# Attention by whole tiles, keys in pairs, and weights, zeros and G moved in a fused attention and mixture kernel

## The chip, the core and the metric

The kernel runs on one core of a Trainium2 chip. The metric is the device time of one execution in microseconds, the median of three runs. PE is the matmul engine, PEld its weight load, DVE the vector engine, ACT the activation engine, POOL the general engine, and SP the engine whose queue issues most of the DMA transfers.

## The reference

All data are fp32. Attention has 2 batches, 8 heads, 768 tokens a batch and 64 channels a head; a query sees 8 global keys and its own last 96, with a bias that falls with the distance. Its output is, as 1536 tokens of 512 channels, the input of a soft mixture of 8 experts with 4 slots each, and the result of that goes through a top-2 mixture of 8 experts with a noisy gate.

```python
scores = np.where(keep, scale * q @ k.T + bias, -1e9); a = softmax(scores); x = a @ v      # heads joined
logits = x @ phi                                                    # soft mixture, 32 slots
d = softmax over tokens; slot_input = d.T @ x
slot_out[e] = relu(slot_input[e] @ w1[e]) @ w2[e]                   # 512 -> 1024 -> 512
x = softmax over slots (logits) @ slot_out
noisy = x @ w_gate + log1p(exp(x @ w_noise)) * noise                # top-2 mixture
top2 = two largest of noisy, weights by softmax
out[mask] += top2_w * (relu(x[mask] @ w1[e]) @ w2[e])               # 512 -> 1024 -> 512
```

## The kernel before

**Attention** works on 12 tiles of 128 tokens. A tile has 4 pairs of heads and is done as two blocks i of two pairs. The loop of `attention_near` runs over the 24 blocks and 3 more turns; in turn i it does scores and exponentials of block i, values of block i - 2 and the turn (transposes) of block i - 1. `scores` (L206) makes four score groups of 167 columns; DVE adds the bias, takes the row's extreme and writes them to SBUF (L209, an eviction); ACT exponentiates them with their sums (`exps`, L216); `norm` adds 1e-9 to the sums on POOL (L222), inverts on DVE (L223) and scales on POOL into Pb (L231, L233); `turn` transposes Pb on PE (L241) and evicts to PT on ACT (L243); `values` multiplies with v (L257); `valued` copies the tile's result to xT on DVE (L264); `stX` transposes it back (L274, copied at L280). After tiles 3, 7, 10 and 11 `logits` (L291) and `seg` (L295 on) bring the last 4, 4, 3 and 1 tiles into a running softmax over tokens: Et, Lsb and rs, transposes at L323 and L324, matmuls at L347, and an update of the sum U (L351).

**Tail.** The last segment's softmax is joined to the others in small steps (L536 to L569): a maximum over partitions, weights Wc, the update of U, then psi = U Wc (L567, "o" in the trace) and siT, the soft experts' input.

**Soft experts.** The weights come as 32 units of 1 MB, four an expert (two of w1a, two of w2a). Units 0 to 15 are loaded in halves during attention; `more_w` with `PACE` (L371) sets how many have been issued by which turn. Units 16 to 31 follow (L616). An expert is `ffn_a` (h, L652), `ffn_t` (m, L685) and `ffn_b` (y, L698). The order of PE is h of e, then m of e - 1, then y of e - 2.

**Routing.** The output op becomes soT; the top-2 mixture doesn't build its input x but works on slots: x = c @ slot_out, so w1 of an expert is first multiplied by slot_out (`g_mm`, also L652, to "pg"; G = relu's input per soft slot), split into fp16 halves `hi` and `lo` (`g_hi` L830, `g_lo` L833), and spread over partitions (`g_mid`, L843 and L844; `g_end`). K0, K1 and K2 are the first three experts of the top-2 mixture; their G, the gate, the top-2 choice and the places of 24 slots of 128 rows are computed together, by order lists written out by hand. Between them stand matmuls without use that keep PE at work (`warm`, L722). A row table ctab with c and the gate of each token goes to DRAM from POOL's queue (L1152), and `slot_a` gathers the 128 rows of a slot from it (L1254) by an index (gidx, L1396). Slots 0 and 1 are taken directly (`direct`, L1138; `slot_h`, L1121). `slot_t` (L1025) turns the gathered rows, `slot_h` and `slot_y` (L1221) are the expert.

**Rows out.** The output is zeroed by DMA (512 rows during attention, `zero_out` L358, 1024 rows in the routing stretch, `zero` L875), and each slot is added to it by an indirect DMA (L1236).

SP's queue is in order, over 8 semaphore lanes: each transfer waits until the eighth before it has landed. In attention, the soft experts and routing PE, and in attention and routing the other engines too, run in the order in which the program is written.

## Time and profile before

| | us |
|---|---|
| median of three runs | 341.44 (339.24 to 341.98) |
| the profiled execution | 339.79 |
| its span, first to last instruction | 337.8 |
| PE busy | 316.5 (94 %) |
| ACT, DVE, POOL busy | 208.0, 197.8, 136.9 |
| granted clock of PE, mean | 0.983 |
| attention ends, experts begin | about 101, 107.46 |
| soft experts end, slot 2 begins | 143.88, 176.59 |

Times in the trace are us from the first instruction. A row of the timeline gives the start, the busy time of a run of like instructions, engine, line and operation, and in brackets the idle time before and what ended it. [...] Busy time of an engine that isn't waited for costs nothing.

### The profile page before, as it was taken

The page shows a single profiled execution, that of the slowest core. Times are in us where ns is not written, and L with a number is a line of the kernel's source. Part 1 is how long each engine was busy: PE and PEld are TensorE (multiplying, and loading weights), DVE is VectorE, ACT ScalarE, POOL GpSimd, SP SyncE. Part 2 cuts the span into 40 slices and gives each one's busy share as a digit, 9 for nine tenths or more (in the row PEclk, how much of TensorE's full clock was granted, in tenths as well). Part 3 has the DMA queues.
Part 4 walks back from the last instruction along what each step waited for, and adds up shares of the span by engine and source line. Part 5 has one row for each costly group of instructions (what it writes and reads, how often), then busy time and mean ns, then how long its engine had stood idle before and what let it go on. Part 6 is the DMA issues. An engine that isn't in the chain of part 4 may idle for free. (4 is left out here: it accounts for less than half of the span.)

```text
span 337.8 us, 7453 instructions
## 1 busy us (share of the span) xinstructions
PE 316.5 (94%) x2687; PEld 187.2 (55%) x2687; DVE 197.8 (59%) x702; ACT 208.0 (62%) x490; POOL 136.9 (41%) x192
## 2 busy tenths in 40 slices
PE   8999999999978999899979999999999999999990
PEld 3789878878854443254544554545454545544540
DVE  3755655556546200049977696797669396898110
ACT  2788868767822210059938796596878695876320
POOL 4466543644520000021444765463643534533131
PEclk9999999999997899999999999999999999999997
DMA  6999999999999999999968999959998955322353
GB/s 176 260 311 291 301 300 278 300 300 309 315 385 394 395 398 399 389 394 398 397 239 183 335 303 367 290 111 318 328 308 262 317 181 71 39 30 31 46 72 47
DMA packets 49226, 89.25 MB, mean 264 GB/s; under 512 B 3408, under 2 KB 18384, under 8 KB 49184
## 3 DMA queue, kind: packets, MB, share of 16 engines
q1 hardware_dynamic: 44704, 80.79, 73.1%
q0 software_dynamic: 4480, 7.92, 14.4%
q8 instruction: 23, 0.38, 0.5%
q14 instruction: 19, 0.16, 0.1%
HBM read 78.56 MB, written 10.14 MB: 263 GB/s over the span
## 5 line engine op out<-in xcount | busy, mean ns | idle before, releaser
L1221 PE MATMUL y<-w2hl,hh 128*128 128x512 f16 x552 | 125.3, 379 | 0.8 <-ACT w2hl L1232 0.8
L1221 PEld LDWEIGHTS <-hh 128*128 128x128 f16 x552 | 52.5, 98 | 62.4 <-issue 4.0
L216 ACT ACTIVATE Tt<-Tt,nm 128x167 f32<-128x167 f32 x96 | 40.5, 424 | 13.0 <-DVE nm L209 12.2
L1130 DVE SCALAR_TENSOR_TENSOR hh<-h,hh 128x512 f16<-128x512 f32 x46 | 29.6, 684 | 22.3 <-ACT hh L1122 22.3
L1236 POOL DMA_INDIRECT out_y<-ys,sidx x15 | 26.9, 1792 | 26.1 <-ACT ys L1230 13.0
L815 DVE SCALAR_TENSOR_TENSOR w2hl<-w,pm,w2hl 128x1024 f16<-128x1024 f32 x28 | 35.1, 1279 | 1.2 <-issue 0.7
L231 POOL TENSOR_TENSOR Pb<-Tt,r 128x668 f32<-128x668 f32 x24 | 31.2, 1300 | 9.4 <-DVE r L223 9.1
L209 DVE CUSTOM_DVE_ANT_0 Tt<-s,bias 128x167 f32<-128x167 f32 x96 | 26.3, 329 | 14.3 <-PE s L206 14.2
L1254 POOL DMA_INDIRECT cT<-ctab,gidx x25 | 28.4, 1137 | 12.8 <-DVE pm L771 6.3
L206 PE MATMUL s<-kx,qd 128*128 128x167 f32 x192 | 31.6, 307 | 0.5 <-DVE nm L209 0.2
L1122 ACT ACTIVATE hh<-h 128x512 f16<-128x512 f32 x46 | 25.0, 598 | 11.0 <-PE h L1121 11.0
L812 ACT ACTIVATE w2hl<-w,pm 128x1024 f16<-128x1024 f32 x28 | 31.3, 1150 | 0.5 <-DVE pm L771 0.5
L243 ACT ACTIVATE PT<-pt 128x512 f32<-128x512 f32 (+1 forms) x48 | 24.4, 558 | 10.4 <-PE pt L241 10.2
L783 ACT ACTIVATE w2hl<-w 128x1024 f16<-128x1024 f32 x28 | 29.5, 1058 | 1.4 <-DMA w<-in_w2b 1.4
L206 PEld LDWEIGHTS s<-kx,qd 128*128 128x128 f32 x192 | 28.0, 196 | 1.1 <-DVE nm L209 0.5
L1236 POOL DMA_INDIRECT out_y<-c,sidx x7 | 12.2, 1736 | 38.3 <-DVE gsc L1215 7.6
L241 PE MATMUL pt<-c,Pb 128*128 128x128 f32 x176 | 24.4, 280 | 1.1 <-POOL Pb L233 1.0
L257 PE MATMUL px<-PT,vt 128*64 128x128 f32 x352 | 24.5, 279 | 0.0
L241 PEld LDWEIGHTS pt<-c,Pb 128*128 128x128 f32 x176 | 18.9, 141 | 6.9 <-issue 3.0
L257 PEld LDWEIGHTS px<-PT,vt 128*64 128x64 f32 x352 | 18.8, 136 | 4.3 <-issue 3.3
L652 PE MATMUL h<-w,siT 128*32 128x256 f32 x256 | 17.4, 418 | 1.6 <-DMA w<-in_w1a 1.5
L1230 ACT ACTIVATE ys<-y,gsc 128x512 f32<-128x512 f32 x15 | 10.3, 688 | 12.9 <-PE y L1221 12.8
(295 smaller groups left out, 465.2 us busy)
## 6 DMA issues: line engine op xcount, KB each, us to landing
w<-in_w2b SPq DMA_DIRECT2D x14, 1024.0 KB, 13.3
x<-in_w1b SPq DMA_DIRECT2D x12, 1024.0 KB, 13.7
w<-in_w1a SPq DMA_DIRECT2D x16, 512.0 KB, 9.6
w<-in_w2a SPq DMA_DIRECT2D x16, 512.0 KB, 9.7
w<-in_w1a SPq DMA_DIRECT2D x8, 1024.0 KB, 13.7
w<-in_w2a SPq DMA_DIRECT2D x8, 1024.0 KB, 15.5
kx<-in_ka SPq DMA_DIRECT2D x12, 272.0 KB, 7.8
qd<-in_qt SPq DMA_DIRECT2D x24, 128.0 KB, 8.2
```

The costliest lines, as they stand in the source:

```text
L206: nc.tensor.matmul(s[:, t, :], qv[:, p, t, :], kx[:, p, a:a + 167], start=True, stop=True)
L216: nc.scalar.activation(Tt[:, k], Tt[:, k], AF.Exp, bias=nm[:, k:k + 1], scale=-1.0, accum_out=st[:, k:k + 1])
L231: nc.gpsimd.tensor_tensor(wide(Pn, 33, 264 + 64, 528, 167), Pu.rearrange("p (a t) c -> p a t c", t=2), rb(167), ALU.mult)
L241: nc.tensor.transpose(pt[:, ch, t], Pn[:, 2 * (n % 2) + t, 136 * ch:136 * ch + 128], ident)
L257: nc.tensor.matmul(px[64 * h:64 * h + 64, p, :], vv[:, c:c + 64], PT[:, ch, :, 64 * h:64 * h + 64], start=(ch == 0 or m == 0), stop=(ch == 1))
L783: nc.scalar.activation(w2hl[:, self.r, 1, 2 * q:2 * q + 2], self.quarter(q), AF.Abs, accum_out=self.wm[:, q:q + 1])
L812: nc.scalar.activation(w2hl[:, self.r, 0, 2 * q:2 * q + 2], self.quarter(q), AF.Copy, scale=self.sw)
L815: nc.vector.scalar_tensor_tensor(w2hl[:, self.r, 1, 2 * q:2 * q + 2], self.quarter(q), self.sw, w2hl[:, self.r, 0, 2 * q:2 * q + 2], ALU.m ...
L1130: nc.vector.scalar_tensor_tensor(hh[:, 1, 4 * q:4 * q + 4], phs[q], 0.0, hh[:, 0, 4 * q:4 * q + 4], ALU.max, ALU.subtract)
L1221: nc.tensor.matmul(py, hh[:, hx, f], w2hl[:, e, wx, f], start=(n == 0), stop=(n == 23))
L1236: o = nc.gpsimd.indirect_dma_start(out=out, out_offset=bass.IndirectOffsetOnAxis(ap=sidx[:, j:j + 1], axis=0), in_=ys, in_offset=None, com ...
L1254: nc.gpsimd.indirect_dma_start(out=cgf[:, place(n)], out_offset=None, in_=ctab, in_offset=bass.IndirectOffsetOnAxis(ap=gidx[:, n:n + 1], a ...
```

## The change

1. The attention loop runs over whole tiles T. Within a tile, the two blocks' scores and exponentials are done, and ACT's evictions of the transposes of tile T - 1 stand one by one among the exponentials (`turn(..., True)` hands back the eviction). The values of tile T - 1 follow at the tile's end. PT has 4 buffers for 2. r is computed on DVE.
2. Keys of tiles 2 to 11 come in pairs of tiles, so rows of 1088 B for 544 B. Values are loaded a tile later.
3. w2a and w2b are read with two rows of weights in a row (4 KB per partition for 2 KB); the halves of h are laid out to match.
4. No zeros are written in attention; one late transfer from 128 partitions writes all 1536 rows (512 and 1024 rows from 64 partitions before).
5. The constants of the first load are cut to 260 columns; the rest comes with the gate's weights and the noise in one later load.
6. In the tail the last tile's part is added to psi in PSUM by four matmuls instead of through U; all engines run in written order; three warming matmuls are added. The splitting of c into fp16 (`halves`) moves into the soft experts.
7. In routing K1's G is computed whole before the first place where G is used, in the bank of K0's; K2's G moves up to the direct slots; the table is written from SP's queue, with the loads of K2's w2b behind it.

```diff
-PACE = lambda i: 1 + 4 * i // 3
+PACE = lambda i: 1 + 3 * i // 2
...
-        w2r = d["w2a"].rearrange("e (c p) f -> e p c f", p=128)
+        w2r = d["w2a"].rearrange("e (c p i) f -> e p c (i f)", p=128, i=2)
...
-        def load_k(T):
+        def load_k(T, n=1):
             a = KP + KS * (T % 6)
-            nc.sync.dma_start(out=kx[:, :, a:a + KS], in_=d["ka"][T].rearrange("p (a t) -> p a t", a=4))
+            nc.sync.dma_start(out=kx[:, :, a:a + n * KS], in_=d["ka"][T // 2][:, :, KS * (T % 2):KS * (T % 2 + n)])
...
-            nc.gpsimd.tensor_scalar(r, st, 1e-9, None, ALU.add)
+            nc.vector.tensor_scalar(r, st, 1e-9, None, ALU.add)
...
-            PT = lo.tile([128, 2, 2, 128], F32, name="PT", bufs=2)
-            nc.scalar.activation(PT[:, c0:], pt[:, c0:], AF.Copy)
-            X["PT", n] = PT
+            PT = X["PT", n] = lo.tile([128, 2, 2, 128], F32, name="PT", bufs=4)
+
+            def out():
+                nc.scalar.activation(PT[:, c0:], pt[:, c0:], AF.Copy)
+
+            if later:
+                return out
+            out()
...
+            for T in range(NT + 1):
+                new, b0, b1 = T < NT, 2 * T, 2 * T + 1
...
                 if new:
-                    more_w(PACE(i))
-                s1 = segs.get(T - 2) if u else None
+                    more_w(PACE(b0))
+                    st0, nm = [sm.tile([128, 4], F32, name=k, bufs=3) for k in ("st", "nm")]
+                    scores(b0, nm)
+                    exps(b0, st0, nm, (0, 1))
...
+                outs = [turn(n, True) for n in (2 * b0 - 4, 2 * b0 - 3)] if T else []
+                for k, o in enumerate(outs):
+                    o()
+                    if new:
+                        exps(b0, st0, nm, (2 + k,))
...
+                    scores(b1, nm)
+                    norm(b0, st0)
+                    exps(b1, st, nm, (0,))
...
+                outs = [turn(n, True) for n in (2 * b1 - 4, 2 * b1 - 3)] if T else []
+                for k, o in enumerate(outs):
+                    o()
+                    if new:
+                        exps(b1, st, nm, (1 + k,))
+                if new:
+                    exps(b1, st, nm, (3,) if outs else (1, 2, 3))
...
+                if T:
+                    for n in range(2 * b0 - 4, 2 * b0):
                         values(n)
...
+        def joined(c):
+            nc.tensor.matmul(psi[:, c, :], U[:, 128 * c:128 * c + 128], Wc, start=(c == 0), stop=False)
...
         for c in range(4):
-            tc.keep_in_program_order(nc.tensor.matmul(psi[:, c, :], U[:, 128 * c:128 * c + 128], Wc, start=True, stop=True))
-        warm(2)
...
+            nc.tensor.matmul(psi[:, c, :], xl[:, 128 * c:128 * c + 128], Ek[:, P1], start=False, stop=(c == 3))
...
         def zero(a, b):
-            nc.sync.dma_start(out=out[a:b].rearrange("(p t) c -> p t c", p=64),
-                              in_=zt[0:64].unsqueeze(1).to_broadcast([64, (b - a) // 64, 512]))
+            nc.sync.dma_start(out=out[a:b].rearrange("(p t) c -> p t c", p=128),
+                              in_=zt.unsqueeze(1).to_broadcast([128, (b - a) // 128, 512]))
...
-        warm(5)
+        warm(2)
+        K1.g_mm(of=K0)
...
-        K1.g_mm((0, 1))
...
-            nc.gpsimd.dma_start(out=ctab.rearrange("(p t) c -> p t c", p=128), in_=crow.bitcast(F32))
+            nc.sync.dma_start(out=ctab.rearrange("(p t) c -> p t c", p=128), in_=crow.bitcast(F32))
+            K2.u.update({i: load_part(2, i, part(stage, i)) for i in (2, 3)})
...
         pct = direct(z)
+        K1.g_pow_a()
+        K2.g_mm((0, 1), of=K0)
...
         h0 = slot_h(0, t01[:, 0:128], scratch([128, 2, 8, 128], F16))
-        K1.g_mm((2, 3))
+        K2.g_mm((2, 3))
...
-        zero(ZREST, NTOK)
+        zero(0, NTOK)
...
-        K1.g_pow_b()
-        K1.g_hi()
-        K1.g_lo()
-        K2.g_mm()
         K1.g_out(0, pm_([128, 2, 256]))
```

ACT in attention, before, two tiles' blocks in the middle (Tt holds a block's scores, nm its row extremes, st its sums, pt the transposes):

```order
L216 ACTIVATE Tt_971,st_969<-Tt_971,nm_970 128x167 x4
L243 ACTIVATE PT_999<-pt_994 128x512
L243 ACTIVATE PT_1006<-pt_1001 128x512
L216 ACTIVATE Tt_1021,st_1019<-Tt_1021,nm_1020 128x167 x4
L243 ACTIVATE PT_1056<-pt_1051 128x512
L243 ACTIVATE PT_1063<-pt_1058 128x512
```

The same engine after, one tile (the blocks 1002 and 1034):

```order
L209 ACTIVATE Tt_1002,st_1000<-Tt_1002,nm_1001 128x167 x2
L238 ACTIVATE PT_1020<-pt_1015 128x512
L209 ACTIVATE Tt_1002,st_1000<-Tt_1002,nm_1001 128x167
L238 ACTIVATE PT_1026<-pt_1021 128x512
L209 ACTIVATE Tt_1002,st_1000<-Tt_1002,nm_1001 128x167
L209 ACTIVATE Tt_1034,st_1032<-Tt_1034,nm_1033 128x167
L238 ACTIVATE PT_1056<-pt_1051 128x512
L209 ACTIVATE Tt_1034,st_1032<-Tt_1034,nm_1033 128x167
L238 ACTIVATE PT_1062<-pt_1057 128x512
L209 ACTIVATE Tt_1034,st_1032<-Tt_1034,nm_1033 128x167 x2
```

The pair of evictions after four exponentials has become four single evictions, each between two exponentials.

SP's queue in routing, before (w2hl<-in_w1b and in_w2b are K2's units, c the row table's tile; the table is on POOL's queue here):

```order
L667 DMA w_1990<-in_w2b 128x4x512
L667 DMA w_1992<-in_w2b 128x4x512
L667 DMA x_2019<-in_w1b 128x2x1024
L667 DMA x_2021<-in_w1b 128x2x1024
L667 DMA w_2065<-in_w2b 128x4x512
L667 DMA w_2067<-in_w2b 128x4x512
L667 DMA w2hl<-in_w1b 128x2x1024 x2
L667 DMA w2hl<-in_w2b 128x4x512 x2
L1403 TENSOR_LOAD go
```

SP's queue there after:

```order
L718 DMA w_1986<-in_w2b 128x2x1024
L718 DMA w_1988<-in_w2b 128x2x1024
L718 DMA x_2015<-in_w1b 128x2x1024
L718 DMA x_2017<-in_w1b 128x2x1024
L718 DMA w2hl<-in_w1b 128x2x1024 x2
L718 DMA w_2064<-in_w2b 128x2x1024
L718 DMA w_2066<-in_w2b 128x2x1024
L1210 DMA ctab<-c_1688 128x864
L718 DMA w2hl<-in_w2b 128x2x1024 x2
L1466 TENSOR_LOAD go
```

K2's w1b units are ahead of K1's w2b now, and the table stands between K1's and K2's w2b; SP waits there until the table's tile is written.

PE between slot 1's values and slot 2's transpose, before (pg is G, the rows L843 and L844 are K1's g_mid):

```order
L1221 MATMUL y<-w2hl,hh 128x512
L652 MATMUL pg<-w2hl,soT 32x256 x16
L843 LDWEIGHTS w2hl
L843 MATMUL m<-ghi,w2hl 128x256
L844 LDWEIGHTS w2hl
```

PE there after:

```order
L1284 MATMUL y<-w2hl,hh 128x512
L901 LDWEIGHTS w2hl
L901 MATMUL m<-ghi,w2hl 128x256
L902 LDWEIGHTS w2hl
L902 MATMUL m<-glo,w2hl 128x256
```

The 16 matmuls of K2's G (twice that in the trace) are gone from this place; they stand in two halves of 8 around `slot_h` of slot 0.

## Rows read from the trace of the kernel before

**Rows 1.** PE's row of the page: busy tenths in 40 equal slices of the span.

```profile
PE   8999999999978999899979999999999999999990
```

**Rows 2.** Windows: us, length, busy time (instructions) by engine, clock, DMA share, GB/s.

```profile
32.58:39.40 6.82, 6.82 (x70) 6.13 (x69) 3.85 (x20) 5.64 (x21) 4.04 (x7) 1.00 1.12 302
...
100.00:110.00 10.00, 9.04 (x57) 5.26 (x58) 6.27 (x21) 1.82 (x6) 0.81 (x3) 0.74 1.04 397
```

**Rows 3.** Timeline of a plain tile, ACT, then DVE: start, length, line, idle before.

```profile
33.90 0.43 ACT L216 ACTIVATE Tt<-Tt,nm 128x167 f32<-128x167 f32 x1 [0.41 <-DVE nm L209]
...
36.04 1.08 ACT L243 ACTIVATE PT<-pt 128x512 f32<-128x512 f32 x2 [0.35 <-PE pt L241]
...
33.47 0.33 DVE L209 CUSTOM_DVE_ANT_0 Tt<-s,bias 128x167 f32<-128x167 f32 x1 [0.46 <-PE s L206]
...
36.02 0.18 DVE L223 RECIPROCAL r<-r 128x4 f32<-128x4 f32 x1 [0.85 <-POOL r L222]
...
38.59 0.69 DVE L264 COPY xT<-px 128x512 f32<-128x512 f32 x1 [0.40 <-PE px L257]
```

**Rows 4.** Timeline of attention, PE: the pieces behind idle time.

```profile
45.77 0.30 PE L323 MATMUL psl<-c,Et 128*128 128x128 f32 x1 [0.42 <-DVE Lsb L320]
...
60.83 1.09 PE L241 MATMUL pt<-c,Pb 128*128 128x128 f32 x8 [0.56 <-POOL Pb L233]
...
97.83 0.27 PE L323 MATMUL psl<-c,Et 96*128 96x96 f32 x1 [1.78 <-DVE rs L326]
```

**Rows 5.** Timeline of the tail and the soft experts, PE, last its weight load.

```profile
104.77 1.91 PE L567 MATMUL o<-Wc,U 128*128 128x32 f32 x8 [0.49 <-DVE U L351]
...
107.46 5.65 PE L652 MATMUL h<-w,siT 128*32 128x256 f32 x64
...
131.69 0.44 PE L685 MATMUL m<-c,hs 128*128 128x128 f32 x2
...
136.65 1.07 PE L652 MATMUL h<-w,siT 128*32 128x256 f32 x16 [1.50 <-DMA w<-in_w1a]
...
137.65 0.44 PE L685 MATMUL m<-c,hs 128*128 128x128 f32 x2
...
140.24 3.64 PE L698 MATMUL y<-w,hT 128*32 128x512 f32 x32
...
142.41 0.13 PEld L698 LDWEIGHTS y<-w,hT 128*32 128x32 f32 x4 [0.30 <-DMA w<-in_w2a]
```

**Rows 6.** DMA packets of three stretches: 20 to 60, 110 to 140, 177 to 190 us.

```profile
DMA packets 10018, 12.07 MB, mean 302 GB/s; under 512 B 570, under 2 KB 6532, under 8 KB 10011
...
DMA packets 4714, 11.85 MB, mean 395 GB/s; under 512 B 347, under 2 KB 347, under 8 KB 4711
...
DMA packets 1286, 2.64 MB, mean 203 GB/s; under 512 B 95, under 2 KB 95, under 8 KB 1286
```

**Rows 7.** Timeline of routing and the loop, PE, with DVE and POOL for the gather.

```profile
154.89 1.24 PE L722 MATMUL y<-c 128*128 128x512 f16 x5
...
161.18 0.61 PE L1121 MATMUL h<-w2hl,Gst 128*128 128x128 f16 x8 [0.52 <-DVE w2hl L1172]
...
173.84 1.93 PE L652 MATMUL pg<-w2hl,soT 128*32 128x256 f32 x32 [1.70 <-issue]
...
176.59 0.22 PE L1025 MATMUL m<-k,cT 128*128 128x128 f16 x1
...
220.69 1.07 PE L652 MATMUL pg<-x,soT 128*32 128x256 f32 x16 [0.53 <-DMA x<-in_w1b]
...
169.42 0.17 DVE L1396 TENSOR_SCALAR gidx<-m 128x25 int32<-128x25 f32 x1
...
172.66 1.05 POOL L1254 DMA_INDIRECT cT<-ctab,gidx  x1 [6.32 <-DVE pm L771]
```

**Rows 8.** DMA issues of the page: KB each, median us from issue to landing.

```profile
out_y<-w2hl SPq DMA_DIRECT2D x1, 2048.0 KB, 12.9
...
ctab<-c POOLq DMA_DIRECT2D x1, 432.0 KB, 6.2
```

More of the change, by code (lines that the diff above doesn't have):

```diff
@@ L99, in load_unit @@
             tv = pl.tile([128, 2048], F32, name=nm, tag=nm).rearrange("p (c f) -> p c f", c=n)
-            units[k] = tv
+            units[k] = tv if not which else tv.rearrange("p c (i f) -> p (c i) f", i=2)
             c = n // parts
@@ L297, in seg @@
             P = slice(0, 32 * w)
-            last = t0 + w == NT
-            hand = near and not last
+            late = near and w < 4
             old, nm = rn
@@ L439, in attention_near @@
-                if s1:
-                    list(s1)
-                if u == 0 and T - 2 in SEGS and T - 2 < NT - 1:
-                    segs[T - 2] = seg(*SEGS[T - 2], logits(*SEGS[T - 2]))
-                if 0 <= i - 1 < NB:
-                    for n in (2 * (i - 1), 2 * (i - 1) + 1):
-                        turn(n)
-                if new:
-                    norm(i, st)
-                if u == 0 and T - 2 in segs:
-                    next(segs[T - 2])
-                    next(segs[T - 2])
@@ new lines, in attention_near @@
+                if T == 0:
+                    tables(0, 0, 2)
+                fill(FILL.get(T, 0))
+                if old:
+                    next(old)
+                if new and 0 <= T - 2:
+                    stX(T - 2)
+                if old:
+                    next(old)
+                if new and T - 2 in SEGS:
+                    segs[T - 2] = seg(*SEGS[T - 2], logits(*SEGS[T - 2]))
+                if T - 2 in SEGS:
+                    next(segs[T - 2])
+                if new:
+                    norm(b1, st)
@@ L455, in attention_near @@
             more_w(2 * (NWA + NW))
+            old = segs[T - 2]
+            fill(1, ps_t.tile([128, 512], F32, name="pt"))
+            next(old)
+            next(old)
+            fill(1, ps_t.tile([128, 512], F32, name="pt"))
             psl = logits(*SEGS[NT - 1])
+            next(old)
+            next(old)
             stX(NT - 1)
             s_hand.close()
-            return psl
+            return psl, old
         def attention_any():
@@ L538, in warm @@
             for _ in range(k):
-                tc.keep_in_program_order(nc.tensor.matmul(pw, warmw[:, 0:128], warmw[:, 0:512], start=True, stop=True))
-        steps = seg(*SEGS[NT - 1], psl)
-        next(steps)
+                nc.tensor.matmul(pw, warmw[:, 0:128], warmw[:, 0:512], start=True, stop=True)
+        s_tail = ExitStack()
+        s_tail.enter_context(tc.manual_schedule(engines=hands))
+        P1 = slice(0, 32)
+        old, nm = rn
+        nc.vector.tensor_copy(nm, old)
+        mx = sm.tile([128, 1], F32, name="mx", bufs=2)
@@ L551, in emit @@
-        next(steps)
+        nc.scalar.activation(wun, old, AF.Exp, bias=mneg, scale=-1.0)
+        nc.scalar.activation(Et[P1], psl[P1], AF.Exp, bias=mneg[P1], accum_out=sg[P1])
+        Wc = cw.tile([128, 32], F32, name="Wc")
+        nc.vector.tensor_scalar(Wc, sel4[:, 0:32], wun, None, ALU.mult)
         sw = cw.tile([128, 1], F32, name="sw")
         nc.vector.tensor_tensor(sw, wun, rs, ALU.mult)
-        Wc = cw.tile([128, 32], F32, name="Wc")
-        nc.vector.tensor_scalar(Wc, sel4[:, 0:32], wun, None, ALU.mult)
@@ L556, in emit @@
-        next(steps)
+        siT = mid.tile([128, 4, 32], F32, name="siT")
+        psi = ps_o.tile([128, 4, 32], F32, name="o")
+        def joined(c):
+            nc.tensor.matmul(psi[:, c, :], U[:, 128 * c:128 * c + 128], Wc, start=(c == 0), stop=False)
+        joined(0)
+        pe = ps_s.tile([128, 2, 128], F32, name="s")
+        nc.tensor.transpose(pe[:, 0, P1], Et[P1], ident[P1, P1])
+        nc.vector.tensor_copy(Ek[:, P1], pe[:, 0, P1])
+        nc.vector.tensor_tensor(sw[P1], sw[P1], sg[P1], ALU.add)
@@ L608, in ph_, with cut32 @@
             return ps_h.tile(shape, dt, name="h")
[L610 to L611 removed]
+        more = cs2.tile([128, 260 + NSLOT + 1], F32, name="more")
+        def cut32(a, n):
+            return more[:, a:a + n]
+        wgn = cut32(0, 64).rearrange("p (c e) -> p c e", c=4)
+        noise = cut32(64, 96).rearrange("p (t e) -> p t e", t=NT)
+        padrow, ovth, below = cut32(160, 1), cut32(161, 72).rearrange("p (e k) -> p e k", e=8), cut32(233, 8)
+        sltm, quarter, spare = cut32(241, NOV), cut32(259, 1), cut32(260, NSLOT + 1)
         for k in range(NWA + NW, 32):
@@ L909, in emit @@
         K0.g_mm()
+        K2 = raw[2] = Rank(2, {i: load_part(2, i, part(stage, i)) for i in (0, 1)})
         K1.u.update({i: load_part(1, i, ring(i)) for i in (2, 3)})
-        K2 = raw[2] = Rank(2, {i: load_part(2, i, part(stage, i)) for i in range(4)})
         warm(3)
```

243 lines of the change are left out of this document (124 added, 119 removed).

## The prediction

> **What bounds the kernel now.** I read the slices of the span first, then the windows, then single stretches of the timeline. [rows 1] show PE at nine tenths or more in nearly all 40 slices, so time is won only where PE idles, does work that need not be there, or runs at a lower clock. The windows [rows 2] say that a plain attention tile takes 6.82 us, every bit of it PE, with ACT busy 5.64 beside it. [...] So three places can give time: the idle pieces inside attention, the stretch from attention's end to the end of the soft experts (clock and data), and the routing stretch. From 185 us on PE is full and its order is the same in both kernels, so a gain made before that is kept to the end, if nothing there arrives late.
>
> **The change part by part**, against the profiled execution's own 339.79 us (span 337.8). The median of the three runs is 1.65 higher.
>
> *Attention by whole tiles.* PE's work per tile is the same, so first the idle time. In [rows 4] PE idles 0.56 for Pb from POOL (once more alike, 0.45 at 18.00), 0.42 for Lsb (once more alike at 75.43), and 1.78 before the third segment's transposes. The change puts a whole turn of the other half tile between a block's exponentials and its transposes, and the segment's steps further apart, so all 3.63 should go. In their place comes a loop on ACT and DVE. ACT's order per tile is now e e P e P e | e P e P e e (e an exponential, P an eviction of transposes), and DVE has r and its reciprocal of the second block, the xT copy, and only then the next tile's first score eviction. r waits for the last exponential, and behind it wait xT and the next evictions, for which ACT waits. Around the loop, from [rows 3]: 0.43 from the first eviction's start (33.47) to the first exponential (33.90); seven exponentials at 0.43 and four evictions at 0.50 (two take 1.08) make 5.0; the last exponential 0.52 with the read of its sum; r and reciprocal 0.42 with two hand-overs, an estimate from the reciprocal's 0.18 for each; xT 0.61 of its 0.69. Sum 6.98 against PE's 6.82. I take 0.15 more for each of the five tiles that have no logits or segment work on PE (in the others PE is longer): +0.7. The ends: nothing (PE still sets the tile) and 8.66, which is a rival below. Attention: -2.9. Moving r to DVE takes 0.22 off POOL, which has 4 of 6.82 us busy [rows 2]; nothing.
>
> *The tail.* From attention's last matmuls to the first expert the chain now runs through the update of U (PE waits 0.49 for it at 104.77) and eight instructions for psi that take 1.91, at the low clock [rows 5]. The change adds the last tile in PSUM instead: no wait for U, but four more matmuls behind the four, and three or so warming ones. -0.5, -0.95 for psi at full clock, +0.85 for what is added: -0.6. Ends: -1.4 (the additions lie beside the softmax chain) and +0.9 (the clock stays low). That the clock stays up is a choice: before it fell, PE idled 1.78 at 97.83 and did scraps of work until 104.7, and the change removes that idle piece and fills others.
>
> *Soft experts.* Now 107.46 to 143.88 (140.24 + 3.64): 36.4 us [rows 5]. The first 64 instructions take 5.65 at the low clock where 32 of the same form take 1.93 [rows 7], so 1.8 is lost. The experts' m matmuls come every 3.95 us (127.74, 131.69), so the next would come at 135.64 and came at 137.65: 2.0 of waiting for w1a, and 0.3 for the last w2a unit at 142.41. Without these 32.3: -4.1.
>
> *Is the data there?* In the new time the second half of the last expert's h matmuls needs its unit 7.0 us sooner than it now arrives (136.65), and the last quarter of the last expert 7.6 sooner than 142.41. [Rows 6] give the stream's prices: from 20 to 60 us 10018 packets carry 12.07 MB, from 110 to 140 us 4714 carry 11.85. Splitting 16 engines' time into a part per packet and a part per byte, 640 = 10018 a + 12.07 b and 480 = 4714 a + 11.85 b engine-us, a is 0.029 us. Keys: ten tiles in five pairs make 2560 packets of 1088 B of 5120 of 544 B, so 2560 x 0.029 / 16 = 4.6 us less. Early zeros: 2048 packets of 512 B cost at least their bytes (1.05 MB at 395 GB/s, 2.7 us) and at most the two-part price (5.6, with b = 0.029 us per KB); I take 3.9, since they are writes and no row has them alone. Second weights with 4 KB packets: 256 packets fewer in each of 16 units, by the two-part price 0.46 us a unit; but in the second stretch, where both kinds of unit alternate, 1 MB takes 2.65 at 395 GB/s, and the last two w2a units took 2.88 each (136.65 to 142.41, the wait's delay in it), so the difference may be small; between 0 and 0.46 I take a third, since the price comes from far smaller packets: 2.6. Together 11.1, so 3.5 to 4 to spare, and PE sets the time. [...]
>
> *Routing.* Here [rows 7]. K2.g_mm leaves its place with 1.70 of idle time before it and 1.93 of work: -3.63. K1.g_mm comes whole behind the prefix matmul (+1.93) in place of three of five warming matmuls (-0.74), and its first half leaves the place before the direct slots (-1.0). K2's first half goes behind them (+1.0), where PE idles 0.52 now. K2's second half takes the place of K1's. Sum -3.0. Late next is the gather of slot 2's rows: issued at 172.66, 3.2 us after its index (169.42), because the row table, written while four units were under way, took 6.2 to land [rows 8]. Now the table goes ahead of two of these units on SP's queue; if it takes half as long, gather 2 goes out at about 169.8 and the slot's transpose, 3.93 behind it as now, can start at 173.7 in the old time, where PE is there at 173.6. Ends: -3.6 and 0. The wait that SP takes for the table delays K2's w2b units, needed only in the expert loop; the c16 split moved into the expert stretch lies on ACT and DVE beside a PE with 3.95 us of work per expert; smaller constants: nothing to 0.2.
>
> *Late zeros and the loop.* 3.1 MB of zeros instead of 2.1, from 128 partitions. Now the 64-partition write runs at 203 GB/s [rows 6], 12.9 us to landing [rows 8]. Behind it come expert 3's units and then those for which PE waits 0.53 at 220.69 [rows 7]. At 395 GB/s the zeros take 8.0, 2.3 less than 2.1 MB at 203; at 203 they take 15.5. No row shows a large write from 128 partitions; reads into 128 partitions run at 395, so I take 8.0, and the 0.53 goes: -0.5. [...]
>
> Sum: -2.9 - 0.6 - 4.1 - 3.0 - 0.5 = -11.1: 328.7 by the profiled execution, 330.3 by the median. I put the forecast between the two: **329.5**.
>
> **The rivals** (each on the same scale).
> - The clock falls again between attention and the experts, since the tail stays a chain of small steps: 1.8 + 0.95 come back, 332.3. For: the drop now comes with just these scraps. Against: less idle time. 0.15.
> - The stream stays the bound. With nothing from the keys 6.5 of 7.6 are won: 330.6; with the low end of the other terms too (2.7 and 0) 4.9 are missing: 334.4. Packets at their bytes' price alone would do it; [rows 6] speak against. 0.12.
> - The late zeros go at 203 GB/s: 5.2 more for the units behind them, and PE waits 5.7 at the place of the 0.53: 335.2. 0.09.
> - Routing keeps its length, since the gather or DVE's chain, not PE, sets slot 2: 332.5. This is also what is left if moving G does nothing. 0.09.
> - **Slower:** the loop on ACT and DVE pays each hop. Now ACT waits 0.41 for DVE and 0.35 for PE's transposes once per half tile [rows 3]; interleaved, it can wait for PE before each of four evictions. 5.5 of work, 2 x 0.41, 4 x 0.35 and 0.94 back through r and xT make 8.66 a tile: ten tiles 18.4 later, less 3.6, the rest -8.2: 347. It ends above before from 8.0 a tile on. Against: the transposes of the tile before can be done long before their place on ACT, since four PT buffers and a step's lead stand between. 0.07.
>
> My case has 0.48; its own range is 326 to 332.5 (loop at 6.82 and the tail's lower end on one side, the gather's on the other). The other cases end at 330.6 to 335.2, so 325.5 to 336 leaves out 0.17 to 0.2. One per cent, about what runs of this kernel can tell from no change, is 338.0 to 344.9: a loop half-way to the slower rival (7.5 a tile) would still give 335, so faster 0.86, same 0.07, slower 0.07.
>
> **What would show it.** Right: PE full in plain tiles of 6.8 to 7.1 us; no 1.78 gap; the granted clock 1.00 from 100 to 120 us; no wait of PE for w1a or w2a; the experts in 32.3 us; no gap before slot 2's transpose; the zeros landing within 9 to 11 us. Wrong: a gap of PE once per tile that ends on DVE's evictions; waits for units of the first experts, because loads now hang on buffers that free themselves later; a slot that waits for its gather behind the zeros.

## Result: 335.4 us, in the range, but under half of the gain

The changed kernel takes **335.42 us** (median of four, 334.62 to 336.41), the kernel before 340.34 beside it; the ratio is 0.9866 [0.9817, 0.9914]. The forecast was 329.5, in a range of 325.5 to 336. So the direction and the range held and the size did not: 5 us came of 11.1. Ratios compare fast runs alone, and of the profiles below one, that of x12, is of a slow run.

The profiled execution (334.62, span 332.8) is 5.0 shorter than that of before, so the two traces can be laid side by side. Each line is the start of the same piece of work in both, and the gain made between it and the line above:

| | before | after | gain of the stage | forecast |
|---|---|---|---|---|
| last logits | 100.02 | 98.28 | 1.74 | 2.9 |
| first expert (L652, now L703) | 107.46 | 104.93 | 0.79 | 0.6 |
| 32-column transposes behind the experts (L726, now L779) | 144.39 | 137.85 | 4.01 | 4.1 |
| slot 2's transpose (L1025, now L1083) | 176.59 | 171.57 | **-1.52** | 3.0 |
| end of the span | 337.8 | 332.8 | 0.0 | 0.5 |

Tail and experts came as forecast. Routing lost 1.5 where 3.0 were to be won, and attention is 1.2 short. The table lays one profile beside one: in x9, the same changed kernel profiled again, the last logits start at 99.50 and routing loses 0.9.

The page's slices of PE and of its clock, which answer to [rows 1]:

```profile
PE   7999999999899999997989999999999999999990
...
PEclk9999999999999999999999999999999999999997
```

Windows of the changed kernel (columns as in [rows 2]): a plain tile, 100 to 110 us, the routing stage, and 173 to 180 us with the late zeros:

```profile
33.06:39.79 6.73, 6.73 (x70) 6.21 (x69) 4.08 (x23) 5.38 (x21) 3.55 (x6) 1.00 1.09 349
...
100.00:110.00 10.00, 9.61 (x121) 6.21 (x122) 5.87 (x21) 3.23 (x9) 0.81 (x3) 1.00 0.98 362
...
137.85:171.57 33.72, 29.53 (x280) 15.73 (x280) 25.50 (x123) 23.54 (x45) 9.92 (x19) 1.00 0.85 330
173.00:180.00 7.00, 6.22 (x44) 3.48 (x43) 5.32 (x14) 6.22 (x11) 4.36 (x4) 1.00 1.03 376
```

A plain tile is 6.73 (6.82), all of it PE. The granted clock, a share of full speed, stays at 1.00 in this profile from 100 to 110 us (0.74 before). The routing window has 4.2 us without PE. The timeline of attention, ACT at a plain tile's start, then PE where it waits, which answers to [rows 3, 4]:

```profile
39.79 0.43 ACT L209 ACTIVATE Tt<-Tt,nm 128x167 f32<-128x167 f32 x1 [1.35 <-DVE nm L202]
...
58.82 0.66 PE L272 MATMUL o<-c,xT 128*128 128x128 f32 x4 [1.03 <-DVE U L344]
...
88.10 0.66 PE L272 MATMUL o<-c,xT 128*128 128x128 f32 x4 [0.81 <-DVE U L344]
...
91.44 0.66 PE L272 MATMUL o<-c,xT 128*128 128x128 f32 x4 [0.79 <-DVE xT L262]
...
94.53 1.06 PE L234 MATMUL pt<-c,Pb 128*128 128x128 f32 x8 [0.40 <-ACT PT L238]
```

The ACT and DVE loop, forecast at 6.97 a tile, has time left: ACT waits 1.35 for the next tile's scores. But the 3.63 of idle pieces in [rows 4] have come back as the four waits shown and one of 0.18, 3.2 together, at other places. The windows from the first scores to the last logits, before, then after:

```profile
6.88:100.02 93.14, 88.94 (x896) 74.58 (x895) 53.44 (x264) 67.90 (x249) 46.91 (x81) 1.00 1.08 302
```

```profile
6.76:98.28 91.52, 87.81 (x891) 75.42 (x891) 57.26 (x284) 64.86 (x250) 41.55 (x57) 1.00 1.04 324
```

PE idles 4.20 in the first and 3.71 in the second. So of the 1.74 only 0.5 is idle time; 1.1 is PE's own busy time, about 0.09 in each tile, and 0.1 the earlier start.

PE in the tail and the experts, which answers to [rows 5]:

```profile
101.97 0.41 PE L590 MATMUL o<-Wc,U 128*128 128x32 f32 x2 [0.39 <-DVE sw L585]
...
104.93 3.66 PE L703 MATMUL h<-w,siT 128*32 128x256 f32 x64
...
131.11 0.44 PE L736 MATMUL m<-c,hs 128*128 128x128 f32 x2
...
133.33 0.44 PE L736 MATMUL m<-c,hs 128*128 128x128 f32 x2
133.70 3.64 PE L749 MATMUL y<-w,hT 128*32 128x512 f32 x32
```

The first 64 matmuls take 3.66 (5.65), no wait for w1a or w2a is left, and the experts take 32.4 (104.93 to 137.34; forecast 32.3). The DMA packets of 20 to 60, 110 to 135 and 173 to 180 us [rows 6]:

```profile
DMA packets 7357, 13.29 MB, mean 332 GB/s; under 512 B 571, under 2 KB 4466, under 8 KB 7349
...
DMA packets 2749, 10.20 MB, mean 408 GB/s; under 512 B 173, under 2 KB 301, under 8 KB 2747
...
DMA packets 1321, 2.63 MB, mean 376 GB/s; under 512 B 43, under 2 KB 43, under 8 KB 1321
```

In 40 us of attention 13.29 MB come in for 12.07, in a quarter fewer packets. The routing stage, which answers to [rows 7]: PE, then ACT, DVE and POOL.

```profile
137.85 1.08 PE L779 MATMUL m<-c,w 128*128 128x32 f32 x8 [0.51 <-ACT w L769]
...
148.87 1.07 PE L703 MATMUL pg<-x,soT 128*32 128x256 f32 x16
150.20 1.07 PE L703 MATMUL pg<-x,soT 128*32 128x256 f32 x16 [0.26 <-DMA x<-in_w1b]
151.86 0.27 PE L901 MATMUL h<-ghi,w2hl 128*128 128x256 f16 x1 [0.59 <-ACT ghi L888]
...
171.57 0.23 PE L1083 MATMUL m<-k,cT 128*128 128x128 f16 x1 [1.65 <-DMA cT<-ctab,gidx]
...
151.34 0.47 ACT L888 ACTIVATE ghi<-pg,pm 128x256 f16<-128x256 f32 x1 [3.00 <-PE pg L703]
...
153.24 0.16 DVE L847 TENSOR_REDUCE wx<-wm 128x1 f32<-128x4 f32 x1 [2.96 <-ACT w2hl L839]
...
166.58 0.17 DVE L1458 TENSOR_SCALAR gidx<-m 128x25 int32<-128x25 f32 x1
...
167.04 1.19 POOL L1317 DMA_INDIRECT cT<-ctab,gidx  x1 [5.43 <-DVE w2hl L1459]
```

Here is the failure. The change writes K1's g_mm (the two rows at L703) ahead of K0's g_hi, in the other half of the same PSUM tile pg (`g_mm(of=K0)`). ACT's read of K0's half (L888) then waits 3.00 until K1's last matmul is through. Behind it on ACT stands L839, DVE waits 2.96 for that, and on DVE hang the index (166.58) and the gather (167.04). Then it is 4.53 from the gather's issue to slot 2's transpose, and PE waits 1.65 of it. Whether the memory itself makes ACT wait, or the order kept for the one tile that both halves belong to, no run shows.

### The profile page after: what moved, and what is told of

Its sections match the earlier page's. It is cut to its first block, busy times and chain, and to the rows that moved or that the text cites. A ratio compares the mean times of both kernels' runs of the same rounds, so it can differ in the third digit from the quotient of the medians.

```text
span 332.8 us, 7416 instructions
## 1 busy us (share of the span) xinstructions
PE 312.3 (94%) x2694; PEld 186.9 (56%) x2694; DVE 201.2 (60%) x724; ACT 205.0 (62%) x490; POOL 134.0 (40%) x167
## 5 line engine op out<-in xcount | busy, mean ns | idle before, releaser
L1317 POOL DMA_INDIRECT cT<-ctab,gidx x25 | 31.1, 1245 | 11.9 <-issue 5.7
L202 DVE CUSTOM_DVE_ANT_0 Tt<-s,bias 128x167 f32<-128x167 f32 x96 | 26.1, 328 | 13.3 <-PE s L199 11.7
L199 PE MATMUL s<-kx,qd 128*128 128x167 f32 x192 | 32.7, 313 | 0.7 <-DMA qd<-in_qt 0.5
L839 ACT ACTIVATE w2hl<-w 128x1024 f16<-128x1024 f32 x28 | 29.5, 1059 | 0.0
L238 ACT ACTIVATE PT<-pt 128x512 f32<-128x512 f32 (+1 forms) x48 | 26.0, 546 | 4.5 <-PE pt L234 4.5
L234 PE MATMUL pt<-c,Pb 128*128 128x128 f32 x176 | 25.2, 276 | 0.7 <-ACT PT L238 0.6
L234 PEld LDWEIGHTS pt<-c,Pb 128*128 128x128 f32 x176 | 20.3, 141 | 3.4 <-ACT PT L238 2.4
L255 PE MATMUL px<-PT,vt 128*64 128x128 f32 x352 | 22.1, 276 | 0.1
L209 ACT ACTIVATION_READ_ACCUMULATOR Tt<-Tt,nm 128x1 f32 x96 | 18.5, 193 | 0.0
```

Source lines behind the costliest of these rows:

```text
L199: nc.tensor.matmul(s[:, t, :], qv[:, p, t, :], kx[:, p, a:a + 167], start=True, stop=True)
L209: nc.scalar.activation(Tt[:, k], Tt[:, k], AF.Exp, bias=nm[:, k:k + 1], scale=-1.0, accum_out=st[:, k:k + 1])
L234: nc.tensor.transpose(pt[:, ch, t], Pn[:, 2 * (n % 2) + t, 136 * ch:136 * ch + 128], ident)
L255: nc.tensor.matmul(px[64 * h:64 * h + 64, p, :], vv[:, c:c + 64], PT[:, ch, :, 64 * h:64 * h + 64], start=(ch == 0 or m == 0), stop=(ch == 1))
L839: nc.scalar.activation(w2hl[:, self.r, 1, 2 * q:2 * q + 2], self.quarter(q), AF.Abs, accum_out=self.wm[:, q:q + 1])
L1317: nc.gpsimd.indirect_dma_start(out=cgf[:, place(n)], out_offset=None, in_=ctab, in_offset=bass.IndirectOffsetOnAxis(ap=gidx[:, n:n + 1], a ...
```

## Experiments

Ratios are to the kernel before, run beside each experiment, with a 95% interval. Each four of them ran on one chip, where the median of before was 340.26 (x1 to x4), 339.32 (x5 to x8), 341.17 (x9 to x12) and 337.65 (x13 to x16). The changed kernel itself ran again beside x10 to x12 alone (x9), so of the others the stages say more than the ratios; above all of x5 to x8, whose ratios all lie near 1.

**1. Where routing lost its time.** x1_scaled_first writes K1's G behind the steps of K0 that ACT waits for:

```diff
         warm(2)
-        K1.g_mm(of=K0)
         K0.w_abs(2)
         K0.g_hi()
         K0.g_scaled()
+        K1.g_mm(of=K0)
```

> Edit: K1's G matmuls are written after K0's g_hi and g_scaled instead of ahead of them; nothing else moves. Theory A (K0's g_hi on ACT waits for K1's matmuls, which share its bank and are written first; ACT stands 3.0 us, DVE behind it 2.96): both waits fall below 0.6, the direct slots start about 2 us sooner (154.3 to about 152.2), the gather's index 2 to 2.5 us sooner, slot 2's transpose at about 169 instead of 171.6, time 2 to 2.5 us less than the change. Rival B (PE itself stands at K1's matmuls for the second w1b unit, landed at 150.2, with K0's g_mid behind): direct slots move by under 1 us, time within 1 us of the change. Rival C (the gather of slot 2 sets its start by the table's way through DRAM, not by the index): direct slots and index move, slot 2 doesn't, time as the change.

333.17 (332.5 to 336.35), ratio 0.9815 [0.974, 0.9891]. The timeline of ACT, DVE and PE:

```profile
149.80 0.45 ACT L888 ACTIVATE ghi<-pg,pm 128x256 f16<-128x256 f32 x1
...
151.84 0.15 DVE L847 TENSOR_REDUCE wx<-wm 128x1 f32<-128x4 f32 x1
...
170.46 0.23 PE L1083 MATMUL m<-k,cT 128*128 128x128 f16 x1 [1.46 <-DMA cT<-ctab,gidx]
```

ACT's and DVE's waits are gone and the stage is 31.05 long (139.41 to 170.46) for 33.72. x2_after_gmid puts g_mm still later, behind K0's g_mid:

> Edit: K1's G matmuls stand behind K0's g_mid, so neither ACT nor PE meets K1's weights before K0's G is spread. Theory A: as the run before, 2 to 2.5 us less than the change, no more than 0.7 apart from it. Rival B: this one gains 2 us or more over the change while the run before gains under 1. Rival C: slot 2's transpose stays at 171 to 172 although the index comes 2 us sooner.

334.61, ratio 0.9814 [0.9753, 0.9874]; the stage takes 33.16. The gather goes out earlier than in the changed kernel (27.52 into the stage for 29.19), but it takes 5.64 to the transpose:

```profile
173.35 0.23 PE L1083 MATMUL m<-k,cT 128*128 128x128 f16 x1 [2.75 <-DMA cT<-ctab,gidx]
```

x3_G_undone puts the steps of G back to their old places (five warming matmuls, K1's G in halves, K2's G whole before slot 2):

> Edit: the G part alone undone: K1's and K2's G and their scaling stand where they stood before, five warming matmuls again; table on SP's queue, 4 KB weights, attention, tail and zeros as in the change. Theory A: moving G up cost more than it gave, so slot 2's transpose comes at about 170.0 (the old 176.6 less the 6.5 by which the soft experts end sooner), time 1 to 1.5 us less than the change. Rival (the move gave its 3.6 and something else in routing lost it): slot 2 at 174 or later, time 2.5 us or more above the change.

338.8, ratio 0.9982 [0.9946, 1.0019]. The stage is 32.20 long, to the digit that of before, but the time is not what was expected:

```profile
170.39 0.22 PE L1083 MATMUL m<-k,cT 128*128 128x128 f16 x1
175.97 1.01 PE L1179 MATMUL h<-ct,Gst 128*128 128x128 f16 x8 [3.64 <-ACT ct L1086]
...
174.67 0.60 ACT L905 ACTIVATE Gst<-m 128x512 f16<-128x512 f32 x1 [7.65 <-remote]
```

Behind slot 2 stands a new wait of 3.64 that ends on ACT's copy of G, and the granted clock falls there (0.72 in the window of 174 to 177 us, 0.71 in that of 177 to 180). What kept ACT for 7.65 is not shown (in x12 below, with the same old order of G, ACT waits 3.13 for PE before this copy), so this run says how long the old order of the stage is, and not what the old order costs.

**2. The weights beside the gather.** The 1.46 left in x1 is the gather, which runs beside K2's last two 1 MB units. x4_w2_behind (on x2) moves both behind the first gathers:

> Edit: as x2_after_gmid, and K2's two w2b units are loaded behind the first two gathers instead of right behind the table. If the gather's 4.5 us from issue to PE's start come from sharing the rings with these 2 MB, it falls to 3.5 or less and slot 2 starts another 0.5 to 1.5 us sooner than in x2; if they are the gather's own, slot 2 is as in x2 and the units come later for nothing. Rival: the late units are missed in the loop, a new wait for w2b of 1 us or more and time above x2.

337.18, ratio 0.9921 [0.9885, 0.9957]. The stage falls to 30.25, and the wait moves to a later slot:

```profile
168.96 0.22 PE L1083 MATMUL m<-k,cT 128*128 128x128 f16 x1
...
178.44 0.23 PE L1083 MATMUL m<-k,cT 128*128 128x128 f16 x1 [1.80 <-DMA cT<-ctab,gidx]
```

Later units are late as well (0.95 at 216.33). x5_units_ahead (on x1) moves both units ahead of the table instead:

> Edit: x1_scaled_first, and K2's two w2b units stand ahead of the table on SP's queue (right behind K1's w2b, as before the change) instead of behind it. Theory D (the gather of slot 2 takes 4.3 to 4.5 us because these 2 MB, released by the table, run with it on the rings; with them out of the way it took 2.7 in x4): the units land before the table is written, issue to PE's start of slot 2 falls from 4.3 to 3 us or less, PE waits under 0.5 there, slot 2's transpose 29.6 to 30 us behind L779 (31.05 in x1, 33.7 in the change), and none of the late waits of x4; time 1 to 1.5 us less than x1. Rival: the units aren't through when the table is written (as before the change, where the table took 6.2 us), slot 2 later than in x1.

336.62, ratio 0.9952 [0.9887, 1.0018]. The table is late now, as the rival had it, but slot 2's transpose is not later than in x1 (30.70 into the stage for 31.05). POOL and PE:

```profile
169.01 1.31 POOL L1317 DMA_INDIRECT cT<-ctab,gidx  x1 [6.56 <-DMA ctab<-c]
...
171.86 0.23 PE L1084 MATMUL m<-k,cT 128*128 128x128 f16 x1 [1.10 <-DMA cT<-ctab,gidx]
```

The next four are the changed kernel once more (x9_change), x1 once more (x10_scaled_first), x1 with one unit ahead of the table and one behind (x11_units_split), and the change with its whole routing part undone (x12_routing_undone):

> The change as it is, on the chip of the three runs beside it, so that they have it as their measure. Expected: L779 to slot 2's transpose 33.7 us, PE's wait for the gather 1.5 to 1.7, ratio to before 0.985 to 0.995. If the granted clock falls between attention and the soft experts, as it did in x1, x5, x6 and x8 and not in x2, x3 and x4, the first 64 matmuls take about 5.2 instead of 3.7 us.

> x1_scaled_first once more, beside the change on one chip: only the order of K1's G and K0's g_hi and g_scaled differs. Theory A: L779 to slot 2's transpose 31.0 us against 33.7, time 2 to 2.7 us less than the change. Rival: what is won before slot 2 is lost behind it (gathers, units), time within 1 us.

> As x10_scaled_first, and of K2's two w2b units one stands ahead of the table and one behind it. Theory D: half the 2 MB delays the table by about 2.5 us less than in x5 (gather issued within 0.6 of its index), the other half the gather less than in x1 (issue to PE's start under 4 us): slot 2's transpose 30.0 to 30.5 behind L779, time 0.5 to 1 us less than x10. Rival: either of them is as slow as with both, no gain.

> The whole of the change's routing part undone (G as before, table on POOL's queue, K2's units behind K1's in one go); attention, tail, packets, zeros as in the change. If x3's stall (3.6 us at the expert matmuls of slot 2) came from the units behind the table, it is gone here, L779 to slot 2 is 32.2 as before the change and the time about 1.5 us less than the change: then the routing part as it was written cost time. Rival: the stall is here too and the time is 2 us or more above the change.

```diff
+        K2.u[2] = load_part(2, 2, part(stage, 2))                    # x11, ahead of the table
...
-            K2.u.update({i: load_part(2, i, part(stage, i)) for i in (2, 3)})
+            K2.u[3] = load_part(2, 3, part(stage, 3))                # x11, behind it
```

x9: 336.31, 0.9862 [0.9801, 0.9924]. x10: 333.48, 0.9764 [0.9703, 0.9824]. **x11: 332.79 (332.44 to 335.38), 0.975 [0.9693, 0.9807].** x12: 336.53, 0.9834 [0.9765, 0.9904]: with the routing part undone the kernel is as fast as with it. On this one chip the order alone is worth 2.8 by the medians (x10 against x9); x11 is not clear of x10 in time. In x11 POOL and PE read:

```profile
169.17 1.19 POOL L1318 DMA_INDIRECT cT<-ctab,gidx  x1 [5.44 <-DVE w2hl L1460]
...
171.87 0.23 PE L1084 MATMUL m<-k,cT 128*128 128x128 f16 x1
```

Slot 2's transpose has no wait; the one two slots later waits 0.76 for its gather. From the 32-column transposes to slot 2, split at the first gather's issue:

| | to the gather's issue | from there to the transpose | stage |
|---|---|---|---|
| before / x12, routing undone | 28.27 / 28.41 | 3.93 / 3.82 | 32.20 / 32.23 |
| change / x9, again | 29.19 / 28.75 | 4.53 / 4.33 | 33.72 / 33.08 |
| x2, G after g_mid | 27.52 | 5.64 | 33.16 |
| x1 / x10, G after g_scaled | 26.71 / 26.72 | 4.34 / 4.39 | 31.05 / 31.11 |
| x5, x1 with both units ahead | 27.85 | 2.85 | 30.70 |
| x4, x2 with both units behind | 27.53 | 2.72 | 30.25 |
| x11, x1 with one ahead, one behind | 26.72 | 2.70 | 29.42 |

**3. Attention.** x6_U_in_s gives the matmuls of U's update the scores' buffers (`pu` from `ps_s` in all segments), so that the transposes at L272 need not wait for it:

> Edit on the change: the segments' four matmuls for U write to the scores' PSUM buffers for all segments, not only the last, so stX needn't wait until DVE has updated U out of the one buffer o. Theory E (of attention's idle time the change gave 3.6 back and took 3.2 in new places, 1.03 and 0.81 of it at stX for U): both waits go, attention ends up to 1.8 us sooner, time 1 to 2 us less than the change. Rival: the scores then wait for the same DVE update (they have two buffers), a new wait at L199 of about the same size, time as the change.

337.62, ratio 0.9998 [0.9945, 1.0051]. The waits for U are gone, and others stand in their place, of which two:

```profile
87.05 0.85 PE L199 MATMUL s<-kx,qd 128*128 128x167 f32 x4 [0.79 <-DVE nm L202]
90.21 0.84 PE L199 MATMUL s<-kx,qd 128*128 128x167 f32 x4 [0.79 <-DVE nm L202]
```

x13_U_earlier leaves the buffers and moves DVE's update of U ahead of the second block's score evictions:

```diff
+                if T - 4 in held:
+                    list(held.pop(T - 4))
                 if new:
...
                     scores(b1, nm)
                     norm(b0, st0)
                     exps(b1, st, nm, (0,))
-                if T - 4 in held:
-                    list(held.pop(T - 4))
```

x14_split_U adds this move to x11, x15_one_more_warm adds a fourth warming matmul in the tail to x14, and x16_units_split is x11 again:

> The changed kernel with one thing moved: DVE's update of U stands ahead of the second block's score evictions instead of behind them and r, at the two places in the loop where PE waits 1.03 (58.82) and 0.81 (88.10) for it. Theory E (the new waits of attention come from DVE's order and are lost time): both waits go, the last logits start 1.5 to 1.9 earlier than 98.28, and the time falls by the same 1.5 to 1.9. Rival (the loop on ACT and DVE takes the time back): the 0.7 of the update delays the score evictions, PE's next scores wait for nm as they did with pu in the scores' buffers, and the last logits stay within 0.4 of 98.28; the time stays.

> The fastest version so far (G of K1 behind K0's scaled splits, one unit of K2's w2b ahead of the table and one behind) with the update of U moved in the same way. Theory E: 1.5 to 1.9 below that version, ratio to before about 0.970. Rival: the same as that version, ratio about 0.975.

> As the one before it, with a fourth warming matmul in the tail where PE idles 0.39 for Wc. If that idle piece is what lets the clock fall between attention and the experts, the granted clock stays 1.00 from 100 to 115 us and the time is 0.5 to 1 lower (1.5 in the half of the runs that have the fall). Rival: the fall is not tied to it; it comes as before in about half of the profiles, and the time is the same or 0.1 to 0.2 longer.

> The fastest version so far once more, beside the two that build on it: ratio 0.975 plus or minus 0.006 on any chip, and 29.4 from the 32-column transposes (L779) to slot 2's transpose, as in the run before.

x13: 334.82, 0.9912 [0.9868, 0.9955], not below the changed kernel. x14: 332.05, 0.9815 [0.9744, 0.9886]. x15: 331.62, 0.9786 [0.9716, 0.9856]. x16: 332.8, 0.9851 [0.9778, 0.9924]. The last three can't be told apart. x16's ratio lies outside what was expected: its time is that of x11 (332.8 and 332.79), but the kernel before is faster on this chip, so ratios from different chips can differ by 0.01. The stage is 29.43 in x16, but 31.05 in x14, where PE waits 1.23 for K1's w1b, and 30.62 in x15, where the table took 5.2 to land (2.8 in x1) and PE waits for slot 2's gather after all:

```profile
170.38 0.23 PE L1084 MATMUL m<-k,cT 128*128 128x128 f16 x1 [1.03 <-DMA cT<-ctab,gidx]
```

PE in x13:

```profile
57.49 0.60 PE L272 MATMUL o<-c,xT 128*128 128x128 f32 x4
...
65.16 1.75 PE L255 MATMUL px<-PT,vt 128*64 128x128 f32 x28 [0.21 <-DMA vt<-in_va]
...
73.64 1.75 PE L255 MATMUL px<-PT,vt 128*64 128x128 f32 x28 [0.52 <-DMA vt<-in_va]
...
91.10 0.66 PE L272 MATMUL o<-c,xT 128*128 128x128 f32 x4 [1.04 <-DVE xT L262]
```

Both waits for U (1.84) are gone, here and in x14 and x15, and the last logits start at 97.94, only 0.34 sooner: PE now waits 0.73 for values from DMA, 0.25 longer for xT, and less at smaller places. In x14's profile one wait for values is 1.80. But a wait for values at this place comes without the move too; PE in x9, where U stands as in the change:

```profile
74.43 1.75 PE L255 MATMUL px<-PT,vt 128*64 128x128 f32 x28 [0.63 <-DMA vt<-in_va]
```

In the twelve profiles with the changed kernel's own attention and packets the last logits start between 98.09 (x16) and 102.27 (x10), half of them before 99.3, and PE's waits for loads there vary from 0 to 2.3. The four waits shown above are the same in all twelve. So theory E is not borne out by the times, and the rival, right that the time stays, has its mechanism wrong: the evictions are not late (0.2 of waiting for nm in x13's whole attention). The DMA stream is full through these tiles (share 1.05 to 1.09 in x13's windows from 30 to 80 us) and some of PE's waits end on its loads, but whether it took back what the move freed, or the scatter hides that gain, is not shown.

**4. Packets and zeros.** x7_small_packets loads each tile's keys alone (544 B rows) and w2a in 2 KB packets again:

> Edit on the change: keys of tiles 2 to 11 again one tile a transfer (544 B rows) and w2a again in 2 KB rows; w2b stays at 4 KB. The two were priced at 4.6 and 2.6 us of the stream. By these prices the last w2a unit (now about 134) lands past 139, later than PE needs it (135.9): PE waits 2 to 4 us for units of the soft experts and the time is 2 to 4 us above the change. Rival (small packets cost their bytes only, or the stream has more to spare): no PE wait for w1a or w2a over 0.5, time as the change.

338.32, ratio 1.0012 [0.9947, 1.0076]. PE waits neither for w1a nor for w2a; late are K1's weights (0.27 and 1.49, for 0.26 in the changed kernel), and the clock falls after (0.52 in the window of 154 to 161 us). PE's timeline, the window, and the packets of 20 to 60 us:

```profile
152.45 1.07 PE L704 MATMUL pg<-x,soT 128*32 128x256 f32 x16 [1.49 <-DMA x<-in_w1b]
```

```profile
154.00:161.00 7.00, 6.05 (x32) 4.00 (x35) 4.71 (x28) 6.15 (x13) 0.99 (x3) 0.52 0.95 379
```

```profile
DMA packets 9555, 12.88 MB, mean 322 GB/s; under 512 B 582, under 2 KB 5823, under 8 KB 9548
```

The rate is 322 GB/s. In the changed kernel it is 332 here, and from 310 to 333 in the fifteen other experiments, which have its packets; in 112 to 135 us, where w2a's packets differ, it is 399, for 407 in the changed kernel and 397 to 410 in the fifteen. So packet sizes of 544 against 1088 B and 2 against 4 KB show no difference in rate beyond the scatter.

x8_zeros_64 writes the late zeros from 64 partitions (`p=64`, `zt[0:64]`):

> Edit on the change: the late zeros (3.1 MB) from 64 partitions. If the partitions set the rate, they take about 15.5 us at 203 GB/s where the change has about 10, and the units behind them come 5 us later. Whether that costs time: theory: K3's units have 10 us to spare in the change (186 against 196.6), so PE meets it only at the units after them, if at all: time 0 to 2 us above the change. Rival (the one of the forecast): 5 us later units reach PE in full, a wait of 4 us or more at G of the next expert and time 4 to 5 us above.

340.8, ratio 1.008 [1.0025, 1.0135]. The window of the zeros, and PE:

```profile
173.00:183.00 10.00, 6.79 (x44) 3.66 (x44) 7.52 (x18) 7.92 (x14) 5.76 (x5) 1.00 0.84 171
```

```profile
183.68 0.23 PE L1083 MATMUL m<-k,cT 128*128 128x128 f16 x1 [2.96 <-DMA cT<-ctab,gidx]
...
221.84 1.07 PE L703 MATMUL pg<-x,soT 128*32 128x256 f32 x16 [0.29 <-DMA x<-in_w1b]
```

171 GB/s for 376 (349 over the same 10 us of the profile after). The units behind the zeros are only 0.29 late; the gather of a slot is 2.96 late, a place that neither theory had.

**5. The clock between attention and the experts.** Of 17 profiles with this tail (the changed kernel and the 16 experiments) the clock falls there in 11 and holds in 6, where the first 64 matmuls take 3.66. In x11 it reads 0.50 from 108 to 110 us and in x10 from 110 to 112; at that level the means of the windows of x1, x9, x11 and x15 come to 3.4 us each. The stretch of the first 64 matmuls in x9, the same kernel as the changed one:

```profile
106.15:111.50 5.35, 5.35 (x66) 2.75 (x66) 2.60 (x6) 0.91 (x2) 0.00 (x0) 0.68 0.89 335
```

The 64 matmuls take 3.66 in the profile after and 5.35 here. From the last logits to the end of these matmuls the fall costs 1.5 to 1.7 in the eleven profiles. x15 cut the idle piece in front from 0.39 to 0.17, and the clock fell all the same (1.00 from 100 to 105 us, 0.67 from 105.16 to 110.30). So that piece alone is not what decides; what does stays open, since PE's rows from the last logits to the fall in x9 are those of the profile after.

## Why the prediction was right in direction and wrong in size

*Soft experts (-4.1): right.* 4.01, by the two pieces named: the clock, and the waits for w1a and w2a. *The tail (-0.6): right*, 0.79. The choice that the clock stays up held in the profile after, which is one of 6 in 17, and that is luck: the rival that had 0.15 is the commoner case. It was priced at 1.8 for the matmuls and 0.95 for psi, half of its 1.91, which fits the clock of 0.50 that the profile before shows from 105 to 111 us; in the profiles of this tail the fall costs 1.5 to 1.7 in all, since it comes late and lengthens the tail by 0.23 at most (x11, x16).

*Routing (-3.0): the step that failed*, by 4.5 us (3.9 by x9's profile). It counted the matmuls that PE no longer has at slot 2, put K1's 1.93 in place of warming matmuls, and did not ask who reads the tile into which K1's G is written. PE's busy time in the stage is 29.53 for 29.30, and falls only where the order is put right (28.75 in x1, 28.59 in x11). ACT's read stood behind 2.4 us of matmuls (148.87 to 151.27) whose result it doesn't use, so index and gather moved back (29.19 to the issue for 28.27), PE waits 1.65 at slot 2, and "late next is the gather" came true sooner than priced. x1 takes 2.0 to 2.7 of this back by order alone, and x11 another 1.7 by moving 1 MB away from the gather; 29.42 and, in x16, 29.43 are the 29.2 that the sum forecast for PE (x14 and x15, with the same order and PE waiting, have 31.05 and 30.62). The forecast's own way of the gather did not come: 25.4 to its issue and 3.93 behind it, for 26.72 and 2.70 in x11. The rival that routing keeps its length, because the gather sets slot 2, had the right place and 0.09; x12 shows that the whole part is worth nothing that the times show (336.53, and 336.31 with it).

*Attention (-2.9): mis-sized*, 1.74, and for the most part by luck. The step that failed is that all 3.63 of idle pieces should go: 3.2 of new waits stand in their place, in all twelve profiles. I did not follow U's update in its new order: behind four evictions and r on DVE, with PE's transposes behind it. x13 removes these two waits, and what is left of that in the time is not shown. The 0.7 for the loop on ACT and DVE was a miss the other way: PE still sets the tile (6.73, at least 0.24 under the sum's 6.97), and the slower rival is refuted by the 1.35 that ACT waits. Most of the 1.74 is PE's own busy time, 0.09 a tile, which the sum took as unchanged. And the profile after is an early one: by the middle of the twelve, 99.3, the gain is 0.7.

*Is the data there?* The outcome was right, the reason wrong. The experts had their data, but with small packets they have it too (x7). By the forecast's price (0.029 us a packet and 29 us a MB) x7's 742 packets a MB would come at 317 GB/s and the changed kernel's 554 at 355; they came at 322 and 332, the latter inside a scatter (310 to 333) that holds both. The price per packet, an estimate, is not borne out: the two stretches that it came from differed in more than packet size, the first with attention's keys, queries, values and halves of units, the second with whole units. What then freed the 3.5 to 4 to spare was not tried alone; the early zeros, whose writes left the stream, and the new issue order of the units (`PACE`), which the prediction left out, are parts that x7 doesn't undo.

*Late zeros (-0.5): rate right, gain not there.* 376 GB/s for the assumed 395, though 11.7 us to landing (x16) are past the 9 to 11 that were to show it. The wait of 0.53 went, one of 0.19 came at 234.85, and 0.0 reached the end. In the stretches with the late zeros the rates were 203 (before) and 171 GB/s (x8) with 64 partitions and 376 with 128.

Sum of the misses: 4.5 + 1.2 + 0.5 - 0.2 + 0.1 = 6.1, the gap of the two sums.

## What to carry to other kernels

When matmuls are moved ahead to fill an engine, look at who reads the tile that they write into: here a reader of the other half, written later in the program, waited 3.00 for them, and with it what stood behind it on its engine, so that DVE waited 2.96; the same matmuls three lines further down are worth 2 to 2.7 us of the stage. An idle piece is won only if the next thing due is early too, so before counting it, list what each engine has queued at the new place, the DMA stream as one of them. A short transfer that someone waits for (a table, a gather) has to be priced with the megabytes that are under way beside it: with two units beside the gather PE waited 1.46 (x1), with both ahead of the table 1.10 (x5), with one on each side not at all at that slot in x11, x14 and x16, and 1.03 in x15. A gain of a stage that is read from one profile has to be held against a second profile of the same kernel: here the end of attention moved by 4 us between profiles of the same code.

## What the runs showed of the hardware

- A read of one half of the PSUM tile pg waited 3.00 for matmuls into the other half (L888 in the profile after); with the matmuls written behind it, 0 (x1).
- The granted clock differed where PE's rows before it were the same: 1.00 in the profile after (104.93 to 108.59) and 0.68 over the like stretch in x9 (106.15 to 111.50).
- Where PE waited 2.75, 3.64 and 2.96 (x2, x3, x8), the mean clock was 0.55 and 0.88 (x2) and 0.72 and 0.71 (x3) in the windows of 174 to 177 and 177 to 180 us, and 0.58 from 184 to 188 (x8). At 0.50, the least that a window shows (x11, 108 to 110 us), that is an estimate of 3.4 us each; in x7, where it was 0.52 from 154 to 161, of 6.7.
- From a gather's issue to its transpose it took 2.70 to 3.17 with 1 MB of weights issued right behind the table (x11, x14, x15, x16) and 4.0 to 5.6 with 2 MB, in the nine profiles where PE waited for it (least in x7, most in x2).
- PE's waits for loads in attention differ between profiles of the same code: none in x8 and x16, 2.2 in x10.
